# New tables for a hand-ordered attention and SwiGLU kernel: order, banks, buffers and block kinds

## The chip, the cores and the metric

The kernel runs on one core of a Trainium2 chip. The core has five engines that run side by side, each through its own instructions in their own order: TensorE (PE in the profile; its weight loads are a row of their own, PEld), VectorE (DVE), ScalarE (ACT), GpSimd (POOL) and SyncE (SP), which here only issues transfers. They wait for each other through semaphores. Matmuls write PSUM, 8 banks of 128 x 512 fp32 words; POOL doesn't touch PSUM here. The metric is the device time of one execution in microseconds; a kernel's time is the median of its runs.

## The reference

An attention block with 32 inducing points over x (4 batches of 12,416 rows of 128 channels), then a SwiGLU feed-forward block with RMS norm over all 49,664 rows, d_ff = 1536, everything in fp32:

```python
def mab(q, kv):
    s = scale * (q @ kv.transpose(0, 2, 1))
    s = s - s.max(-1, keepdims=True)
    a = np.exp(s)
    a /= a.sum(-1, keepdims=True) + 1e-09
    return a @ kv
h = mab(I, x)                      # I: 32 inducing rows
x = mab(x, h).reshape(B * S, D)
...
rms = np.sqrt(np.mean(x * x, axis=-1, keepdims=True) + 1e-06)
xn = x / rms * rms_g
g = xn @ w_gate
silu = g * (1.0 / (1.0 + np.exp(-g)))
val = xn @ w_val
return (silu * val @ w_out).astype(np.float32)
```

## The kernel before

**Tiling.** A batch is cut into 7 sets of rows, six of up to 2,048 rows and a rest of 256. A set makes four units (the last set one), so there are 25 units to a batch and 100 in all: 80 of 512 columns, 16 of 480 and 4 of 256. The feed-forward part takes each unit through 12 blocks of 128 of the 1,536 hidden columns, 1,200 blocks. Since the second attention's output is a combination of 32 rows, the gate and value weights are first multiplied with those rows; a gate is then one matmul of the stack `sg` with the unit's attention weights `a` (L720), a value one with `sv` (L748).

**A block.** After gate and value, ACT takes the silu (L730) and DVE the product u (L762). Then u is projected by `w_out`, and the letter of the block in the table `sorts` says how:

- P: the product is written to a buffer in SBUF and one fp32 matmul takes it with `wo` (L818; the profile has two records for it).
- S: the product stays in its PSUM bank. ACT makes a high half (L775), DVE a low half (L781), PE multiplies both (L806, L807) in fp32r, POOL adds the two halves in place (L826), and a third fp32r matmul takes the sum (L818).
- D: the product goes to SBUF, ACT makes the high half (L772), POOL the low half (L788), ACT scales the high half down (L794); from there on it is as S.

So P costs one fp32 matmul and nothing on ACT and POOL. The first two projections of a unit collect in one bank, the rest in another; at the unit's end ACT scales the one up (E, L850), DVE adds both (F, L859) and turns the result (T, L865), and SP stores it (O, L880).

**Work between.** The attention of the next batch (scores, exponentials, sums, norms: small matmuls L327, L380, L574 and pieces on all engines) and the splitting of `wo` run among the blocks: 879 such pieces. For each unit SP gathers `a` from the halves `hi` and `lo` by four transfers (L658) into one of two buffers.

**What sets the order.** No scheduler: the kernel runs under a manual schedule, and after a hand-written opening (`first()`, its own string ORDER) one string, `program`, is walked letter by letter. A letter issues one step: g gate, v value, s silu, m product, h high, l low, n and e the two steps of D, q the first two projections, d the add, r the third, p the plain projection, a the gather, E F T O the end of a unit, and a dot the next piece by its number in `taken`. The order of the letters is the order of the instructions on each engine's queue; semaphore waits are put in where data or buffers ask for them. Other tables give what a step uses:

- `banks`: the PSUM bank of each matmul group that opens one (2,707 digits);
- `holders`: which of 19 SBUF buffers a product or half is written to;
- `workers`, `outputs`: scratch and output buffers of the attention pieces and units;
- `picks`: where several blocks are ready for a step, which of them is taken (A the oldest);
- `sorts`: the kind of each block.

```python
for name in "".join(program.split()):
    step, args = micros[int(next(taken))] if name == "." else (do[name], ())
    in_turn(step, args, id(step) in alone)
```

Of the kernel before, what the change touches and what calls it, by code (L numbers as in the profile page):

```python
# [23 lines left out]
def kernel(  # L24
# [12 lines left out]
    m = inducing.shape[0]  # L37
# [1220 lines left out]
    def seams():  # L1258
# [13 lines left out]
        5674130256174302653024631602314062310426304162403164026143614302614076214076241036421635260135215603251032512034  # L1272
        5704571042751407523071207310273610276037231627361237013125317247315472150732457125321627536751671236153076513750
        7453451401743052173021735203105705635761760345701547341725702754751047624752370250240542764207560274602174603241
        0217413720546130173051354731703105340571245743673741534367317451267345173461540635613465036154025360432473604727
        0326473261032451605315432463165345276135276135261302601521045165412605264712615246512346521365134526261742601761
        6476201760314270152670524215460245601462135426172436524356124361256134513041035431743517053147037215702170251075
        2674152061274016274016741360713460735140753470254027430723405237020325103203651306521036501620137632431471673123
        6714261670416071504650147514061705642076442034270634207342106321642654235415246532013426031476320763476327064730
        2407230724571437542375142361725375603265103512635026514356031540514675064716501457261724721347261762347162341726  # L1280
        4315643764175610456740132657425764073475345605743650465635031036213251023561703214703475423541305423410654312657
        1643726254632675043742761320614272076471240762406275025472412754173514732512417236124126013264106413624013260170
        6512052761072615072156047214076041743046301367204163216305164654163405163456034576453676534726732574621736275327
        5632563275630216735216302563042150425341052731402531503561026135601236521053245415375241372157431502347570526730
        7536257230652643720413713024037210732471360417630756034540547360543765473267326516571352631075620753245236752437
        6254726342532617301750215621562701250172472401724740371231745027153025673165713051706314507614521404706427014267
        0132704152734527305427304637401256430242341021642361203467341263567517273276531762157036173510365436453140346521
        0341063426712637471426314753164370467136017314036437014703763470243724530734025403257124031234026304632614201423
        6501236047123640723403216234063451673513571567415376413257463521365032162136520165027301706412461741607261072640
        2310742123417341724357124504235142513425164256312574627356024370653047607640375630417045123014521342053126543054  # L1290
        1025745120571412046517604650645076037435043674265720751025615760127510651624756427432576437246537605234653062501
        2306105630246130561735120352063615326143045367436174571345143653712451721724512172014051732410241076103740137163
        4760516470617506270624754704326750365102571370215317207530724302630726037240673245620235062352031026305601253702
        5603672324037463276103412073157412574027120542571602670526375236502765326503715623457617267412542675102745217341
        0314024723107614027164516710612571721067521350263060564234520426730567305273571607516730167350143602156401630320
        3241063247012640162
    """
    workers = """
        20120102102102010120120201201201201201212120120102011021010210210
# [5 lines left out]
        abcdefghiacbedfghiacjklmbdnoegpqfirshacjklmbdgeifacnohpqbilmrsdgjknpefalqomcrjhbiskdgnlapqefoscbnkhriamjdplqogrs  # L1305
        pnfebchaqlkmijpdnogfersqkljmhbpanqiokdrselmjpnqoklfgjcbnphodralqismjknpeorgblqjksmfcnpdolqrijkshnaepolqgmjrkfsnc
        lbiqpomjrdelghaqpcfiksnjrbdhlomnrjaksfqplomncrjgkislbqpmoenkrjdqslpnhmfkacoqsrjmgnklpibsrjemoqndksrljpmoqfhnksrj
        lmapogqsrmcnjpbolkqsnreijomlkpqdhsanrjfcgbiqmeklhpocsdngbrajsiqhmklrepocfnjdbasigecnjqmdklbrposfqamhnkgjlrpcqoes
        njklmqdifbarogpsnlmqjkhrposenlidmqcrpfbosnmglqharjepkfinmcodbpkgsrahefjlqopinbcgsmajrhfqkdolcnjrpasoehbqmgiflkcd
        njrseoqahpmbilkncgdjoqrfsphmnabilkjeoqrspmnlkjogcrdhspfbqmnkaijslorpecqmhfgnrdkpqjabmslonireqckjlpdmofsnhqkgjrbl  # L1310
        apmioqcsknjlrpmdfoqshnjkeglpbsrminaocdfkjhlqspbrmoegdkjnsplrqimhkopjlfcmrnqaskobdlpnjqsmogknrljqepmosikrlhnpcmoa
        jsfqkrnplbmodgejichrsfqnakmbpegolcjqnkrsmpholijrqsnamdepgkobjlfnrcmpjlkhiqsemoanjrkpqlsmognldbsrfckjpqmonlshirka
        jepqmogfsnrcldpkqjmbsrnloqpijskmrnlpaohegqjcdrkonfmsbilpoaehgqjnrfbkmcsoilqjpkmdgsolqnejkpmhrnsoalpqjcmkigrnfesl
        dbhopmqjkarcslgniopfjkedslmqhrnopagjkmbqrcinsfdlojpagqrhkmenscijploqrbfnsdakghicmloebjnfpsadqkrmhljionpgfcqsekrd
        amlhjoibnpfqscekrmldgjonpqsahmlkribfjoqcnsepmlkrdgjoahqnfsrbljokpmqinsecorlkdjpamnqhlfjsgbkoemrpqcinljadskhfgeom
        bcirpqndlskjogqmnrecpkalojsbnrqhpfkmidlognprjcseqakmnplobqsirfdjghalekobmncpjdqsrkoilmgnpjqbrsokfnhpacledimrnsjq
        pokmrlnskmpojqgrnlksmbjpqrfonhlkcadesjpmqrloikngsjbplmqfhroknpmaqsjlrkonpmqsjlodrecinpqmjsklgrjfbosaqhcnmpklrjie
        nqmogdfpskjlcmbonqrkaphlmqerjiosgnkpqldfbcrmojpihlnsqgekrmojpacdfblnsqmokjrphlnsigkqjmloernpsdabjcfhlogiemkdhqrf
        jnpsclogaqremkbjlnodpihfsjqlrpcamkensbojirqfhlpojmkrnqsgoldjpcermankbfijrpmhgqsdoaenlckjbrpmqinsfdlogkjhrpnscmqa
        lobefkjrpinsdmrqpkjlohmrgnsqlpkojnabecmsrojpikqdnlmsrfkhojpnqmrslojkgpnbqrlsomjkcpanlsqeorimjfkpndshoqmlbrkjngps  # L1320
        cameoqplsjifrndhoqkpbmlrsgncjmolkpaeqroslndjmkphqbroislkfnjpmgqroslknacjpmldkqeroisnjbphfgmlkraqsonpjkdrqsmlonpk
        jcrqinfeblposkmrjqnlhgadopskcrjblmqeofnispghkrljqmnaospdlcbjnkrqmoseilpjnqghfamkrojsbnlprmokqcdjiesparfnlmokqbsr
        jpmhognclkeafisqrjnpolbkmsdqcgriojslenapqrkmfhojbsndglpqrckmiojelahspnqrkmojblfsdgnpqmorckjshlinaepobrqmsndlfrqk
        jgcpmhoslnaeriqkbjoslfnrpdmqgksljhaopcmnrkqlesjiopbmnrkfqsgljmdcophnrlajkeqsiopmlbnrjgfhkqsopmcdalnieb
    """
    sorts = """
        PPPPPPPPPPPPPPPPPPPSPSDPDPDPPPSDPPPPPPDDPDPSSPDSPSSDDPDPPDPDSDPDPSPSSPSPSPSSSDSPPDPSSSPSSSPDSPSSSSDDPSSSDSSPSSSS
        SPSDPSSPSSDSSPSDSPPSSSDPDPPDPSSPSPSSSDPSSPSSPSSDSPSSDSSSSPSSDSPPSSSSPSSSSSDSSSSSPSSDSSSSDSSSSDSDDSDPSPSSPSSPSSDD
        PPPPSPDPSSPPSSSPSSSDSPSPSSSDSPPSSSSSDSDPPSPPDSDDPSPPSPPSPSPSPPPPSSSSDPDDPSPSDDPDPPDPDDSPDPPDSPPSSSDPPPSPSSSSSSSD
        SPPPSSDDSPSDPSDSPDSSSSSSDSPPSDSPSSPPSSSSDPSSSPSSDSSDPDSPSSPSDSSSPSSSDSSPSPSSSSSDSSPSPSSSSPSPDSSDPPDDPPSPSSPSDDSS  # L1330
        SSPDSSSPSSDPSPSSSPSPSDSSSPSSSDPSSSSSDPSSSSSSSSSSSSSSSSSDDPSSSPSPDSDPPSSSSPSDSPPSSSSSSPSSDSPPDDPPPSDSDSPSSSPPDSSP
        SSPDSDPPDSPSDPSPDPSSPSPPPSPPPSSSPDPSDSPSDDPDPDSPDPSPDPSPPSSSDPSPDPSSPSSSSPPSDPDSSSSDPSSPSDSSDDSPPSSPSDDPDPPSPSSS
        SSPDSPSSDSSPDSDSPSSSSDSSDPSSPSSPPSSSSSDSDPSSSPPSPSSSSSSSSSPSSSSPSDSPPPPPSSSSPSSDPSPSPSSSDSSSSSSSDDSSPSSSSSPPSSSD
        SSPSSSSSSSSSSSDDSSSDSSPSSDPSSSPPSPSSSSSDSPSSDSSDPDPPPSSPPSDSPPDSSPDSPPSDSDDPSSPPPSPSSSSSPSPSPPPSSPSSPSDPPSPSSDSP
        DPSPSDPSDPDPSPSSDSSPSSPSSSSPPSPSSSPSPSSSSSSSSSSPDSSSPSSSDSPPSSSSSDSSPDPSSSSSDPSSPSSPSSSPSPSSDSSPSSPSSSDSSSPSSSDP
        SPSSDPSSPSSSSSSSSSPSPSDPSSSSSSDSPSPSSSSDPSSSSSSSPSSSDPSSPDPSSPSSSSDPPSSPSSSSDSSSSSPPSSSSDSSSPSSSPSSSSDPSDPSPPSSP
        SDSSSSSPSSSSDSSPSSPSSSSSDPSSPSSSSPSDSSPSSSSPSSSSDPSSPSPSDSPDSSSPSPSSSPPDSSDPPPPP
    """
    picks = """
        ABABAAAAAAAABABABAAAAAAAAAAAAAAAAAAAAAAAAAAAAAABAAAAAAAAAAADCABAAAAAAAAAAAAAAAAAAAAAAAAAAAAAAAABAAAAAAAAAAAAAAAA  # L1340
# [221 lines left out]
```

## Time and profile before

| | us |
|---|---|
| time, median of 3 runs | 1471.8 (1471.11 to 1471.89) |
| the profiled execution's own time | 1469.96 |
| its span, from the first instruction to the last | 1468.1 |
| mean granted TensorE clock | 0.999 |
| first gate of the blocks (L720) starts at | 41.5 |
| last matmul starts at | 1462.8 |

The profile is of one execution. The columns of the view of windows are the stretch, its length, and for each engine its busy time in it with its count of instructions, then the granted clock, the DMA engines' busy share and GB/s. A row of the view of groups gives line, engine, operation, what is written and read, and the count; behind the first bar the busy time in us and the mean ns of one, behind the second the idle time of the engine before it and what ended it. A row of the timeline gives start, duration, engine, line and operation; neighbours of one kind are merged, with their count. Matmul durations overlap, since matmuls are pipelined: the start of the next one shows what one costs.

### The profile page before, as it was taken

The numbers are of one execution on the slowest core, as the hardware profiler recorded it, in microseconds if no ns is written. First come the engines' busy times: TensorE is split into PE (matmuls) and PEld (weight loads), VectorE is DVE, ScalarE is ACT, GpSimd is POOL, SyncE is SP. The second block draws the span as 40 slices with busy tenths as digits, with TensorE's granted clock in tenths as the row PEclk, the third lists the DMA queues.
The fourth block names the chain that finished last, engine by engine and source line by source line (L and its number), as shares of the span: only waits on it lengthen the run. The fifth ranks groups of instructions, "written<-read, shape, count | busy, mean of one in ns | idle before, by whom it ended". The sixth has DMA issues, their size and how long they took to land.

```text
span 1468.1 us, 26087 instructions
## 1 busy us (share of the span) xinstructions
PE 1460.1 (99%) x7310; PEld 1106.3 (75%) x7310; DVE 1427.4 (97%) x2489; ACT 1304.2 (89%) x2607; POOL 1376.3 (94%) x1214
## 2 busy tenths in 40 slices
PE   9999999999999999999999999999999999999998
PEld 7557777877777777787777777787778777777787
DVE  7999999999999999999999999999999999999998
ACT  6798889889988988988999889898898899999987
POOL 2579998999999999899999999799999999999998
PEclk9999999999999999999999999999999999999999
DMA  7656224446444132726656221264322122212122
GB/s 283 137 95 126 55 55 87 113 104 119 90 87 84 25 67 47 150 48 139 112 106 118 39 42 37 49 130 98 62 57 54 33 37 44 39 38 40 37 43 34
DMA packets 391904, 116.02 MB, mean 79 GB/s; under 512 B 365648, under 2 KB 371280, under 8 KB 389200
## 3 DMA queue, kind: packets, MB, share of 16 engines
q1 hardware_dynamic: 391168, 114.28, 37.8%
q8 instruction: 58, 0.95, 0.3%
q14 instruction: 86, 0.70, 0.2%
q10 hardware_dynamic: 592, 0.08, 0.0%
HBM read 53.95 MB, written 27.00 MB: 55 GB/s over the span
## 4 chain that ended last, share of the span: by engine, by line
PE 98%; DVE 1%; ACT 0%; issue 0%; POOL 0%; POOLq 0%; DVEq 0%; ACTq 0%
PE gv L818 32%; PE gv L720 17%; PE gv L748 17%; PE gv L806 12%; PE gv L807 12%; PE gv L327 3%; PE gv L380 1%; PE gv L945 1%; PE gv L574 1%; PE gv L158 0%; PE gv L989 0%; PE gv L468 0%; DVE u L762 0%; ACT silu L730 0%; PE gv L1099 0%
## 5 line engine op out<-in xcount | busy, mean ns | idle before, releaser
L730 ACT ACTIVATE silu<-gv 128x512 f32<-128x512 f32 (+2 forms) x1200 | 675.2, 592 | 79.3 <-PE gv L720 62.7
L826 POOL TENSOR_TENSOR xn<-xn,xn 128x512 fp32r<-128x512 f32 (+2 forms) x468 | 580.7, 1257 | 23.0 <-PE gv L807 20.7
L720 PE MATMUL gv<-a,sg 128*128 128x512 f32 (+2 forms) x1188 | 478.4, 432 | 0.0
L748 PE MATMUL gv<-a,sv 128*128 128x512 f32 (+2 forms) x1188 | 449.4, 411 | 0.0
L762 DVE TENSOR_TENSOR gv<-silu,gv 128x512 f32<-128x512 f32 (+2 forms) x662 | 432.6, 673 | 6.1 <-PE gv L748 2.9
L775 ACT ACTIVATE xn<-gv 128x512 fp32r<-128x512 f32 (+2 forms) x643 | 376.2, 596 | 34.9 <-DVE gv L762 28.3
L762 DVE TENSOR_TENSOR u<-silu,gv 128x512 f32<-128x512 f32 (+2 forms) x538 | 343.1, 655 | 7.6 <-ACT silu L730 3.8
L818 PE MATMUL gv<-u,wo 128*128 128x512 f32 (+2 forms) x708 | 347.8, 577 | 1.2 <-DVE u L762 1.0
L781 DVE SCALAR_TENSOR_TENSOR xn<-xn,gv 128x512 fp32r<-128x512 f32 (+2 forms) x509 | 332.2, 662 | 5.1 <-ACT xn L775 3.0
L720 PEld LDWEIGHTS gv<-a,sg 128*128 128x128 f32 x1188 | 223.4, 189 | 102.2 <-issue 33.2
L748 PEld LDWEIGHTS gv<-a,sv 128*128 128x128 f32 x1188 | 223.0, 189 | 85.4 <-issue 23.1
L826 POOL TENSOR_TENSOR xn<-xn 128x512 fp32r<-128x512 f32 (+2 forms) x200 | 250.8, 1261 | 6.5 <-PE gv L807 6.2
L788 POOL TENSOR_TENSOR xn<-u,xn 128x512 fp32r<-128x512 f32 (+2 forms) x159 | 197.4, 1245 | 7.9 <-ACT xn L772 6.3
L826 POOL TENSOR_TENSOR u<-xn,u 128x512 fp32r<-128x512 f32 (+2 forms) x154 | 194.4, 1271 | 1.9 <-PE gv L807 1.7
L806 PE MATMUL gv<-xn,xn 128*128 128x512 f32 (+2 forms) x451 | 170.2, 378 | 0.0
L818 PEld LDWEIGHTS gv<-u,wo 128*128 128x128 f32 x708 | 132.0, 190 | 30.0 <-issue 12.0
L818 PE MATMUL gv<-xn,xn 128*128 128x512 f32 (+2 forms) x360 | 134.9, 385 | 0.0
L807 PE MATMUL gv<-xn,xn 128*128 128x512 f32 (+2 forms) x360 | 134.5, 374 | 0.0
L806 PE MATMUL gv<-xn,more 128*128 128x512 f32 (+2 forms) x347 | 131.3, 379 | 0.0
L772 ACT ACTIVATE xn<-u 128x512 fp32r<-128x512 f32 (+2 forms) x179 | 110.8, 620 | 9.2 <-DVE u L762 8.4
L794 ACT ACTIVATE xn<-xn 128x512 fp32r<-128x512 f32 (+2 forms) x179 | 112.1, 629 | 4.6 <-POOL xn L788 3.3
L818 PE MATMUL gv<-xn,more 128*128 128x512 f32 (+2 forms) x292 | 112.4, 393 | 0.0
(233 smaller groups left out, 1862.9 us busy)
## 6 DMA issues: line engine op xcount, KB each, us to landing
out_dram<-o SPq DMA_DIRECT2D x320, 64.0 KB, 2.0
xT<-in_x_dram SPq DMA_DIRECT2D x60, 256.0 KB, 4.5
xn<-in_x_dram SPq DMA_DIRECT2D x60, 256.0 KB, 5.2
a<-hi SPq DMA_DIRECT2D x152, 64.0 KB, 2.0
a<-lo SPq DMA_DIRECT2D x152, 64.0 KB, 2.0
xn<-in_x_dram SPq DMA_DIRECT2D x5, 1024.0 KB, 9.2
xn<-w SPq DMA_DIRECT2D x18, 256.0 KB, 4.4
out_dram<-o SPq DMA_DIRECT2D x64, 60.0 KB, 2.0
```

The lines of the kernel that those rows point to most:

```text
L720: nc.tensor.matmul(g[:, 0:T], stacks[b][0][:, ts(j, P)], halves_in_turn(one["a"][:, 0:T]), start=True, stop=True)
L730: nc.scalar.activation(sl[:, 0:T], gates.pop(n)[:, 0:T], AF.Silu)
L748: nc.tensor.matmul(v[:, 0:T], stacks[b][1][:, ts(j, P)], halves_in_turn(one["a"][:, 0:T]), start=True, stop=True)
L762: nc.vector.tensor_tensor(out=to, in0=sl[:, 0:T], in1=v[:, 0:T], op=ALU.mult)
L775: nc.scalar.activation(hi, t["u"], AF.Copy, scale=-(1.0 - 2.0 ** -13) * 2.0 ** -12)
L781: nc.vector.scalar_tensor_tensor(out=t["lo"], in0=t["hi"].bitcast(F32), scalar=4096.0, in1=t["u"], op0=ALU.mult, op1=ALU.add)
L788: nc.gpsimd.tensor_tensor(out=t["lo"], in0=t["u"], in1=t["hi"].bitcast(F32), op=ALU.subtract)
L794: nc.scalar.activation(t["hi"], t["hi"].bitcast(F32), AF.Copy, scale=-(2.0 ** -12))
L806: nc.tensor.matmul(to, weight_of(0, j), halves_in_turn(t["hi"]), start=not one["q"], stop=False)
L807: nc.tensor.matmul(to, weight_of(1, j), halves_in_turn(t["lo"]), start=False, stop=last)
L818: nc.tensor.matmul(to.rearrange("p (n h) -> p h n", h=2) if step2 else to, lhsT, rhs, start=one["left"] == NJ, stop=one["left"] == 1)
L826: nc.gpsimd.tensor_tensor(out=t["lo"], in0=t["hi"].bitcast(F32), in1=t["lo"].bitcast(F32), op=ALU.add)
```

## The change

Only tables change; no function does, nor the opening's ORDER. Compared place by place, these letters differ: `sorts` 32 of 1,200; `banks` 2,393 of 2,707; `holders` 2,082 of 2,207; `picks` 1,186 of 4,694; `workers` 41 of 65; `taken` 706 of 879; `program` 9,838 of 10,871; `outputs` none. The counts of the kinds go from 354 P, 662 S, 184 D to 371 P, 651 S, 178 D. `picks` other than A go from 482 to 865. The sequence of the attention's matmuls on PE and how many of them stand together stay as they were (90 matmul pieces in 53 runs), as does the number of changes between Exp and Silu on ACT (24).

```diff
     banks = """
-        5674130256174302653024631602314062310426304162403164026143614302614076214076241036421635260135215603251032512034
...
+        5674130257461207546740207562375627362703673026357032653260753265723652376513267312670361073631230476130417301472
...
     holders = """
-        abcdefghiacbedfghiacjklmbdnoegpqfirshacjklmbdgeifacnohpqbilmrsdgjknpefalqomcrjhbiskdgnlapqefoscbnkhriamjdplqogrs
...
+        abcdefghibacdefghibjkadelmcfghinoadbpqerscgihafbjkdlmcepqirsnoajlmghfpqdbckreisnahjogcmlpsebkqihrjdnofcgmlpsbenk
...
     sorts = """
-        PPPPPPPPPPPPPPPPPPPSPSDPDPDPPPSDPPPPPPDDPDPSSPDSPSSDDPDPPDPDSDPDPSPSSPSPSPSSSDSPPDPSSSPSSSPDSPSSSSDDPSSSDSSPSSSS
...
+        PPPPPPPPPPPPPPPPPPPSPPDPPPDPPPSDPPPPPPDDPDPSSPDSPPSPDPDPPDPDSDPDPSPSSPSPSPSSSDSPPDPSSSPSSSPDSPSSSSDDPSSSDSSPSSSS
...
     program = """
-        .gg.vs.vg.sgvs.gv.g......m.mspms...s....vv.mp.mpm.g...s..p..g.gsp.....g..gvp.ms.vvs....mp.msg.p....s.vv.vm.p....
-        g.mp..msv.p......gvvmsp.gmg.s...smp...vv....m..p.....ggsp....msvv...p.m.g..g.v..ps.s.av.g.mp.sm.gvm.h..s...l..m.
...
+        .gv.g..gv.s..smsv..gmvsggmvsp...p..v...m.gmsp...vgs.p...sv...pm....gp.s.g..m.mgsvp...s.p..mv.ggmvs..ms.p........
+        vp....mgv.sp.mvvgm..s..g.vv.sp...p...p.m.mg.gsp...mvsvg.g.sp....p..m..vm.v.gsg..pa.s.sgvm....h..ms..l..m..p...v.
...
     taken = """
-        114 4 116 1 0 62 24 88 115 5 87 25 2 3 8 50 26 9 28 6 27 51 113 29 118 53 12 63 52 54 55 10 64 16 30 119 89 11
...
+        115 1 62 116 24 88 0 2 117 8 25 5 120 4 50 26 6 27 3 9 29 28 51 12 30 53 52 113 54 63 114 40 55 64 10 59 65 89
...
```

More of the change, by code (lines that the diff above doesn't have):

```diff
@@ L1276 @@
[L1276 to L1285, printed above, removed]
@@ new lines @@
+        4162431502641506720162514571672142574162753126537253027506253053602540234621426312063120673167203716716425076425
+        0765204240645170263572031025712516270125746105201465314635124351265143256357362576053726072365706352403752305243
+        0514012450317234502375437652476325476352713406135061450614510346356243065264570467502467027467530542147107540270
+        5420174023047324607360472640730764103742025632764256746357421374267236073460324632710431204650435206352340623456
+        0263052537651326157261371453276527150261306315362503614216420160364701647316047603175303450347523502745302457320
@@ new lines @@
+        4701325737235712657342617035237540236037605320376350261370230243607264072653046730164201762012430610625306125046
+        2170215415710541243045370645710535436053401345601450260126316201321073210670326175213215724135723573251473215461
+        0263125360156310562137056235605163561641064350637540130673506306503762056257603524053725172353475132741254705347
+        0143701367014374160375461304257624352647325761437241354315230412341032543012546106170672604270146716230430720154
+        7021570452710746503425302463254302350462653407654071647376376417360137610326317657623761317645127463510375345714
@@ new lines @@
+        3701437105273140764204372137213470147213451341732163764325361475634132407263071603120175623170572034031401745043
+        1754601540751205761027561375310246371267206123061703627135726307450420607650476250746507215267243574365736272641
+        3256375217507653203276250347064750641736105304134365430514603645062456704602475240176450721725072350752701203521
+        7635170653476123076327641627312754607147104126014720642715604271407214037401372134720415201367326136023762037160
+        7162431242716726147625471271634576356137501370635721632067312043760432603204372306542751670562516725612051732670
@@ new lines @@
+        6254062507450620671427504765047652430647364270213074107450375104730435013750241043562134156431256125473257634503
+        7560346054075340760725017456142517256142376523642640726370537602751603750756037047657630734606510572167451674627
+        5421367546725367057640730536503475601532706271560251675602714607430147301763410764120437064375403450673047501674
+        0361073432640372405306357437216375234534751452437014731574561745317456345163407165031732176521720652147502415034
+        5730217015031230265734073502564053542356403160214517560750471576410364103541326503620315601365271023607243704064
@@ L1297 @@
+        0236740524357250673
     """
     workers = """
-        20120102102102010120120201201201201201212120120102011021010210210
+        20120201201201020120121021021020102012020201201201020120111201201
     """
@@ new lines @@
+        csmblkqnjopsfraligdkqmnehjrbfkopqclmagsjdbinrhfepqcksgjabdiolnmphekfcjgiebrpnqacskhmojedbrlifasphmocdfnqkjgrsilb
+        hadpmfoncrskqjleiphagdomrjnkfbqpslormceinjaqghkorsdfmlpqbinjekacromshnjglkpfmqrbsnopimcjldqaegrskmhfbopnjdilqrks
+        onegclbprqmhjsnoapdiflqkgcearjpdniemsokbcrljpnhqafmgrsonkleqmijprcdsbohjprsqkfmljnroasqpeigjkmnsbcpldrohqjksfpal
+        igecmdhbnrfokqcspjhefilomjqnspdkrlhaqgsnmobkpcfrleisjkmpnoqdrapbheslkjropncmqsfpgihklnrabjmosnepqdcifkhjralmpoqk
+        sjnbgdporfqlhkmnscieapqjogbdnhkrmpceqlaisjgnomfbpckehdarmgqslinbfhjoakpqrnmdsjolkngqhfsrecbmpjoiadgklnqsmfcrjopk
@@ new lines @@
+        lebinaghrqsmcodfihjpekliansbcormqhdjkflnpmgieoqlrasncbhdfipjgekolmarcdfpbigsqjnhlraskfipjecqnglhamsfroeipqbgkjln
+        cdmrapsqlfokjeibnghmpcdaqjrolksfbinmdhlrespqokcngidmjlkqbsrfholnaqkespmrcdiojnlhqksbfmgaedorchifnpsqilkjmodnchsg
+        aljqmbpofkrnisedlahqjbfmpkosrdcnlqgjkeohbmpisadcrqnefljibskmoprnqlgafhmjidosnkqprblcheaodmfrsjnqolkpimqhjbleonrk
+        mspqgcjlondmafhierkmsopqjglnbrkcqmosedpjlrfonqkpsmljrpisoqajhnkgbprmecfsqlojnkdispgbfmqjraklhcseifgpmonkjlsqprda
+        bolkmsqgnjioprfsqlkhcaonpregbslmiafqojpknhsdbemrjlqsknpmcogrjaklnqofhpesridbocaghnkfbjmgqlheposnakrbfqljmipkdogs
@@ L1383 @@
+        AAAAAAAAAAAAACCAAAAACAAAAAAAACAAAAAAABAABAAAAAABAAAAABAAAAAABABAAAAABAABAAAAABABAAAAAAAABABBAAACBBAAAA
     """
     program = """
[L1385 to L1387 removed]
@@ L1483 @@
+        shvmgrgsqmhdlphTsrdhgvlrOsqlgvgdqmqlsmvvEvdmrgvmsrhrmgsgpldhmslsqhvgqdhmqslgrhdrlsvqlvgdmqqmsvpFdrpmdTpvdpOmErrr
+        rpprFTO
     """
     taken = """
[31 rows of a table removed]
[31 rows of a table added]
     """
```

337 lines of the change are left out of this document (156 added, 181 removed), and 60 rows, old and new, of the table taken.

## The prediction

> **What bounds the kernel now.** I read the page's first lines, then one stretch of the windows view, from the first gate (41.5 us) to the last matmul (1462.8 us). What lies ahead is the opening, which the tables leave alone; behind it come the last unit's sum, transpose and store.
>
> ```profile
> span 1468.1 us, 26087 instructions
> PE 1460.1 (99%) x7310; PEld 1106.3 (75%) x7310; DVE 1427.4 (97%) x2489; ACT 1304.2 (89%) x2607; POOL 1376.3 (94%) x1214
> PE 98%; DVE 1%; ACT 0%; issue 0%; POOL 0%; POOLq 0%; DVEq 0%; ACTq 0%
> ...
> core 0: us, PE busy (x) PEld busy (x) DVE busy (x) ACT busy (x) POOL busy (x), PEclk, DMA share, GB/s
> 41.50:1462.80 1421.30, 1419.99 (x6840) 1074.76 (x6839) 1396.01 (x2393) 1277.55 (x2546) 1365.00 (x1187) 1.00 0.37 73
> ```
>
> PE is on 98% of the chain at a granted clock of 1.00, but DVE and POOL stand beside it at 97% and 94%. Busy time alone doesn't say whether PE streams or waits, since matmul ends are modelled. The starts do, so next comes the timeline of PE.
>
> ```profile
> 700.12 0.38 PE L720 MATMUL gv<-a,sg 128*128 128x512 f32 x1
> 700.34 0.38 PE L806 MATMUL gv<-xn 128*128 128x512 f32 x1
> 700.56 0.38 PE L807 MATMUL gv<-xn,xn 128*128 128x512 f32 x1
> 700.77 0.38 PE L818 MATMUL gv<-xn,more 128*128 128x512 f32 x1
> ...
> 702.28 1.02 PE L818 MATMUL gv<-u,wo 128*128 128x512 f32 x2
> 702.74 0.78 PE L818 MATMUL gv<-u,xn 128*128 128x512 f32 x1
> 703.36 0.38 PE L748 MATMUL gv<-a,sv 128*128 128x512 f32 x1
> ```
>
> A 512-column fp32r matmul starts (700.77 − 700.12) / 3 = 0.216 us after the one before. From 702.28 to 703.36 lie one plain block (the fp32 matmul with wo, two records) and one fp32r matmul: 1.08 − 0.216 = 0.86 us for the plain block. An S or D block sends three fp32r matmuls, 0.65 us. Narrower units I take by columns (480/512, 256/512).
>
> ```profile
> L720 PE MATMUL gv<-a,sg 128*128 128x512 f32 x948 | 386.0, 436 | 0.0
> L818 PE MATMUL gv<-u,wo 128*128 128x512 f32 x532 | 270.6, 594 | 1.2 <-DVE u L762 1.0
> L818 PE MATMUL gv<-u,wo 128*128 128x480 f32 x138 | 66.6, 566 | 0.0
> L818 PE MATMUL gv<-u,wo 128*128 128x256 f32 x38 | 10.7, 380 | 0.0
> ```
>
> With the widths (960, 192 and 48 blocks of 512, 480 and 256 columns; plain ones 266, 69 and 19, two records each) the block matmuls need 502.9 (gates and values) + 533.8 (S and D) + 292.6 (P) = 1329.3 of the 1421.3 us. The remaining 92 us hold the attention's matmuls and all of PE's waits. Going over all starts behind 41.5 us for those later than this spacing and the switches between tile shapes explain, I count 121 places with 11.2 us together, the first and the last of them here:
>
> ```profile
> 43.82 1.07 PE L327 MATMUL gv<-xT,hT 128*32 128x512 f32 x8
> 45.93 1.13 PE L818 MATMUL gv<-u,wo 128*128 128x512 f32 x2 [1.04 <-DVE u L762]
> ...
> 1462.77 0.19 PEld L818 LDWEIGHTS gv<-xn,more 128*128 128x128 f32 x1 [0.24 <-POOL xn L826]
> 1462.77 0.38 PE L818 MATMUL gv<-xn,more 128*128 128x256 f32 x1
> ```
>
> Sorted by what was late: 2.9 us in 26 places at the third matmul of a block (it waits for POOL's add), 2.2 in 20 at gates, 1.7 in 20 at values, 2.0 in 29 at the first two projections, 1.4 in 18 around plain blocks, and 1.1 in the row at 45.93. So PE streams for all but 0.8% of the span. **The change can gain 11.2 us at most, and pays from that whatever PE gets more to do.**
>
> **The change part by part.** *Block kinds.* Counting the letters: P 354 to 371, S 662 to 651, D 184 to 178; by width 13 more P at 512, 4 at 480, none at 256; by batch +8, +8, +2, −1. Each swap costs PE 0.86 − 0.65 = 0.21 us: 13 × 0.21 + 4 × 0.20 = **+3.5 us**, on the path, as nothing covers work on PE itself. The other engines are relieved, by these rows:
>
> ```profile
> L781 DVE SCALAR_TENSOR_TENSOR xn<-xn,gv 128x512 fp32r<-128x512 f32 (+2 forms) x509 | 332.2, 662 | 5.1 <-ACT xn L775 3.0 <-issue 0.2
> L775 ACT ACTIVATE xn<-gv 128x512 fp32r<-128x512 f32 (+2 forms) x643 | 376.2, 596 | 34.9 <-DVE gv L762 28.3
> L772 ACT ACTIVATE xn<-u 128x512 fp32r<-128x512 f32 (+2 forms) x179 | 110.8, 620 | 9.2 <-DVE u L762 8.4
> L794 ACT ACTIVATE xn<-xn 128x512 fp32r<-128x512 f32 (+2 forms) x179 | 112.1, 629 | 4.6 <-POOL xn L788 3.3
> L788 POOL TENSOR_TENSOR xn<-u,xn 128x512 fp32r<-128x512 f32 (+2 forms) x159 | 197.4, 1245 | 7.9 <-ACT xn L772 6.3
> L826 POOL TENSOR_TENSOR xn<-xn,xn 128x512 fp32r<-128x512 f32 (+2 forms) x468 | 580.7, 1257 | 23.0 <-PE gv L807 20.7
> ```
>
> DVE 11 × 0.66 = 7.3; ACT 11 × 0.60 + 6 × 1.25 = 14.1; POOL 11 × 1.26 + 6 × 2.50 = 28.8 us. None of it lies on the path by itself; it shortens the end only through PE's 11.2 us.
>
> *Weight.* The Trainium skill (TensorE: Matmul & The Clock Gate, section Back-to-back issue gap) gives about 131 ns per 512-column matmul in a sustained stream; a swap, one pass more, would cost 0.13 us by it and the 17 swaps 2.2. The rows above contradict it with 216 ns, so 3.5 stands.
>
> *Order, picks and buffers.* The list's order is the order on each engine. I measure a lead as the time that PE's entries between two places of the list take at the spacing above. The POOL add of a block (L826) stood closer to its third matmul than its own duration in 76 of 846 blocks; now in 25 of 829. The first plain block followed scores2 of set 1 directly; now seven gates and values stand between. A buffer of the 19 comes back to its next writer within 1 us of the matmul that last read it 293 times before, 181 now. Banks don't move: a silu, product, low half, scale_up or finish closer to the next matmul in its bank than its own duration 232 times before, 226 after (scale_up alone 2 and 8). High_down ahead of its projections gets worse, 9 short leads to 15.
>
> *What the waits become.* Row 45.93: its 1.1 us goes to 0 (DVE's product is covered by 7 × 0.216 = 1.5 us). Third matmuls: 2.9 × 25/76 = 1.0. For the other 7.2 us the bounds are 0 and 7.2 or more; I scale by the buffer leads, 181/293, to 4.5, since of their counts this one moves most; by the bank counts alone they would stay at 7.0. Sum 5.5, **a gain of 5.7 us**. What is late next is a gate or value behind its bank:
>
> ```profile
> PEld gv L720 <- ACT silu L730: 15.7, 62, 0.7
> PEld gv L748 <- ACT silu L730: 14.3, 60, 0.4
> PEld gv L818 <- POOL xn L826: 11.3, 36, 0.8
> ```
>
> These are idle times of the weight loads, most of it under a running matmul, so they order the causes and don't price them.
>
> *Table loads.* Going through ACT's entries for Exp and Silu, both lists change between them 24 times, in the same stages.
>
> ```profile
> L730 ACT ACT_TABLE_LOAD x12 | 15.4, 1283 | 1.3 <-PE gv L720 1.1
> L456 ACT ACT_TABLE_LOAD x8 | 10.3, 1283 | 0.1
> L358 ACT ACT_TABLE_LOAD x4 | 5.1, 1283 | 0.1
> ```
>
> 24 × 1.28 us before and after: nothing.
>
> *Transfers.* SP's queue is reordered too. Loads of x for the next batch keep at least 9 us ahead of their transposes. The gathers of a (L658, four transfers) are the exception:
>
> ```profile
> L658 SPq DMA_DIRECT2D a<-hi x192: 507/581/2702, 105.6 to 1439.9; - x192
> DMA to landing us min/median/max: 1.8/2.0/7.9
> ```
>
> Three issues of 0.58 and a landing of 2.0 make 3.7 us. Before, one gather of 98 had less than 6 us to its unit's first gate, now nine have 5.0 to 6.0. I take nothing for it, as 5.0 covers 3.7; the bound on the other side is the longest landing, 1.7 + 7.9 = 9.6, some 4 us late each.
>
> *Sum.* 1468.1 + 3.5 − 5.7 = 1465.9 us of span. This profiled execution took 1469.96 with its 1.9 us around the span, and the median of the runs, 1471.8, lies 3.7 above the span: **1469.6 us**, 0.15% below. A measurement of this kernel tells about 0.2% (2.9 us) from no change, so I forecast no change.
>
> **The rivals.** *Nearly all waits go.* If the relief on POOL and ACT frees the banks as well, some 2.5 of the 11.2 us stay: 1468.1 + 3.5 − 8.7 + 3.7 = 1466.6. For it: every lead count but two falls. Against: the bank counts hardly do. It decides from 6.5 us of waits gone; all gone gives 1464.1, the lowest possible.
>
> *PE isn't full.* PEld is busy 1074.76 of 1421.30 us; if the missing quarter were room, the extra passes of the 17 blocks would run in it and 3.5 would fall out: 1466.1. Against: a load takes 0.19 of the 0.216 us of a matmul, and the two loads of a plain block 0.38 of 0.86, so a full PE shows about this share with this mix. The Trainium skill (Perfetto Trace Analysis, section Identifying the Most-Contended Engine) states the rule behind it, that the busy share of weight loads measures PE's headroom and matmul busy time doesn't; by it the 76% here leave room, and the starts disagree.
>
> *The gathers arrive late: slower.* Place: the first gate of the nine units. If their four transfers take 6.2 us rather than 3.7, because an issue ahead of them on SP waits, PE stands 0.7 us at each: 9 × 0.7 = 6.3, and 1469.6 + 6.3 = 1475.9. It decides from 5.1 us of such waits (0.57 each). Everything on SP queues behind a gather that waits for its buffer, and the stores behind that. Speaks for it: the longest issue 2.70 and landing 7.9 us; against: the medians.
>
> **How the numbers follow.** Forecast 0.40 (its own range 1468.9 to 1474.7, where 7.0 of the other waits stay or a few gathers slip); waits gone 0.33; PE not full 0.05; gathers late 0.22. So faster 0.38, same 0.40, slower 0.22. The range goes from the floor, 1464.1, up to 1476.2, where all 11.2 us of waits stay (1475.3) or the gathers take 6.2 us; about 0.13 lies above it and little below.
>
> **What would show it.** PE should have 34 more wo records, at L818, and 17 fewer at L806; POOL's busy time should be 29 us smaller, ACT's 14. The wait of L818 on POOL L826 should shrink to a third and the one at the first plain block vanish. If gates of a fresh unit wait for DMA, the third rival holds; if PE's late starts stay near 11 us, the leads were not what mattered; if they sum to under 4, the first rival holds. A span that falls although PE's late starts stay would make the sum wrong from the ground up.

## The result, and the profile after

The changed kernel takes 1468.81 us (median of 18 runs, 1467.97 to 1470.39) against 1471.09 us for the kernel before in the same session (18 runs, 1470.27 to 1472.77): ratio 0.9983, 95% interval 0.9976 to 0.999. It is 2.3 us faster. The interval leaves out 1, so the gain is real; at less than 0.2% it lies inside what the prediction called no change. The forecast was 1469.6 us, reckoned from 1471.8 us for the kernel before.

The first lines of the page of the changed kernel and its chain of waits by engine, and behind them the stretch from the first gate to the last matmul in the windows view:

```profile
span 1467.2 us, 25908 instructions
...
PE 1460.5 (100%) x7293; PEld 1109.9 (76%) x7293; DVE 1424.0 (97%) x2478; ACT 1297.0 (88%) x2584; POOL 1351.5 (92%) x1191
...
PE 99%; DMA 0%; DVE 0%; issue 0%; ACT 0%; DVEq 0%
```

```profile
42.79:1461.82 1419.03, 1419.01 (x6823) 1077.21 (x6822) 1392.63 (x2382) 1270.36 (x2523) 1340.29 (x1164) 1.00 0.37 73
```

The span fell by 0.9 us, the stretch by 1421.25 − 1419.03 = 2.2 us: the first gate starts at 42.79 instead of 41.52. I don't count that 1.3 us to the change: the profiled runs of the experiments below, whose tables leave the hand-written opening alone too, have their first gate anywhere from 41.6 to 42.75 us, those that begin with the list of before (kinds_only at 42.75) as well as those that begin with the changed one (more_plain at 41.7). So the stretch is what is compared from here on.

How much of the stretch PE loses is read with one sum. Going down the list, I add up PE's work at the spacings of the prediction (0.216 us for a pass of 512 columns, 0.86 for a plain block, the attention's matmuls at their usual time) and subtract it from the time at which each matmul starts, with the first gate at zero. What grows is **PE's time beyond its stream**: waits, what a wait costs behind it, and odd switches between tile shapes.

| time, us | before | changed |
|---|---|---|
| 60 | 2.7 | 1.4 |
| 100 | 5.2 | 2.6 |
| 160 | 6.5 | 3.7 |
| 500 | 12.1 | 8.0 |
| 1000 | 18.6 | 13.5 |
| end | 23.9 | 18.2 |

At the end it falls by 5.7 us. The change in the stretch is that, with the plain blocks against it: −5.7 + 3.5 = −2.2. Half of it, some 2.8 us, is won before 160 us. The late starts, counted as in the prediction, went from 11.2 us in 121 places to 5.2 in 59: third matmuls 0.7, gates 1.4, values 1.2, first two projections 1.5, plain blocks 0.5.

The place of the first plain block, in the timeline of the changed kernel:

```profile
44.01 1.07 PE L327 MATMUL gv<-xT,hT 128*32 128x512 f32 x8
45.01 0.48 PE L748 MATMUL gv<-a,sv 128*128 128x512 f32 x1
...
46.19 0.38 PE L748 MATMUL gv<-a,sv 128*128 128x512 f32 x1
46.43 1.98 PE L818 MATMUL gv<-u,wo 128*128 128x512 f32 x4
```

The plain block starts 0.24 us behind the value ahead of it, where a pass takes 0.216: the 1.04 us of before are gone. The groups of instructions and the waits of the weight loads answer to those shown before:

```profile
L818 PE MATMUL gv<-u,wo 128*128 128x512 f32 (+2 forms) x742 | 364.6, 577 | 0.0
```

```profile
PEld gv L748 <- ACT silu L730: 11.8, 44, 0.8
PEld gv L720 <- ACT silu L730: 9.7, 40, 0.6
PEld gv L818 <- POOL xn L826: 5.4, 22, 0.4
```

The wo records are 742, 34 more than the 532 + 138 + 38 of before. The weight loads' wait on POOL's add is halved (11.3 to 5.4 us, where a third was forecast), and no gate of the changed kernel waits for a gather. The longest late start of a block's matmul is 0.33 us.

### The profile page after: what moved, and what is told of

It reads as the page before. It is cut to its first block, busy times and chain, and to the rows that moved or that the text cites. A ratio compares the mean times of both kernels' runs of the same rounds, so it can differ in the third digit from the quotient of the medians.

```text
span 1467.2 us, 25908 instructions
## 1 busy us (share of the span) xinstructions
PE 1460.5 (100%) x7293; PEld 1109.9 (76%) x7293; DVE 1424.0 (97%) x2478; ACT 1297.0 (88%) x2584; POOL 1351.5 (92%) x1191
## 4 chain that ended last, share of the span: by engine, by line
PE 99%; DMA 0%; DVE 0%; issue 0%; ACT 0%; DVEq 0%
PE gv L818 33%; PE gv L720 17%; PE gv L748 17%; PE gv L806 12%; PE gv L807 12%; PE gv L327 3%; PE gv L380 1%; PE gv L945 1%; PE gv L574 1%; PE gv L989 0%; PE gv L468 0%; PE gv L158 0%; PE gv L490 0%; DMA ind<-in_inducing_dram 0%; PE gv L567 0%; PE gv L1099 0%
## 5 line engine op out<-in xcount | busy, mean ns | idle before, releaser
L826 POOL TENSOR_TENSOR xn<-xn,xn 128x512 fp32r<-128x512 f32 (+2 forms) x379 | 469.8, 1251 | 19.2 <-PE gv L807 15.6
L720 PE MATMUL gv<-a,sg 128*128 128x512 f32 (+2 forms) x1188 | 462.3, 414 | 0.0
L775 ACT ACTIVATE xn<-gv 128x512 fp32r<-128x512 f32 (+2 forms) x608 | 354.6, 593 | 30.6 <-DVE gv L762 24.8
L818 PE MATMUL gv<-u,wo 128*128 128x512 f32 (+2 forms) x742 | 364.6, 577 | 0.0
L781 DVE SCALAR_TENSOR_TENSOR xn<-xn,gv 128x512 fp32r<-128x512 f32 (+2 forms) x445 | 291.6, 662 | 6.7 <-ACT xn L775 5.1
L826 POOL TENSOR_TENSOR u<-xn,u 128x512 fp32r<-128x512 f32 (+2 forms) x204 | 254.5, 1255 | 7.0 <-PE gv L807 3.7
L806 PE MATMUL gv<-xn,xn 128*128 128x512 f32 (+2 forms) x431 | 172.5, 400 | 0.0
L788 POOL TENSOR_TENSOR xn<-u,xn 128x512 fp32r<-128x512 f32 (+2 forms) x125 | 156.9, 1259 | 10.8 <-ACT xn L772 7.6
L818 PEld LDWEIGHTS gv<-u,wo 128*128 128x128 f32 x742 | 138.2, 190 | 29.5 <-issue 11.8
L806 PE MATMUL gv<-xn,more 128*128 128x512 f32 (+2 forms) x330 | 127.8, 387 | 0.0
L818 PE MATMUL gv<-xn,xn 128*128 128x512 f32 (+2 forms) x304 | 120.5, 404 | 0.0
L807 PE MATMUL gv<-xn,xn 128*128 128x512 f32 (+2 forms) x304 | 113.7, 374 | 0.0
L781 DVE SCALAR_TENSOR_TENSOR u<-xn,gv 128x512 fp32r<-128x512 f32 (+2 forms) x163 | 107.8, 666 | 1.6 <-ACT xn L775 1.0
L772 ACT ACTIVATE xn<-u 128x512 fp32r<-128x512 f32 (+2 forms) x166 | 103.0, 622 | 5.9 <-DVE u L762 4.3
L794 ACT ACTIVATE xn<-xn 128x512 fp32r<-128x512 f32 (+2 forms) x166 | 102.9, 623 | 4.9 <-POOL xn L788 2.9
```

Source lines behind the costliest of these rows:

```text
L720: nc.tensor.matmul(g[:, 0:T], stacks[b][0][:, ts(j, P)], halves_in_turn(one["a"][:, 0:T]), start=True, stop=True)
L772: nc.scalar.activation(hi, t["u"], AF.Copy, scale=1.0 - 2.0 ** -13)
L775: nc.scalar.activation(hi, t["u"], AF.Copy, scale=-(1.0 - 2.0 ** -13) * 2.0 ** -12)
L781: nc.vector.scalar_tensor_tensor(out=t["lo"], in0=t["hi"].bitcast(F32), scalar=4096.0, in1=t["u"], op0=ALU.mult, op1=ALU.add)
L788: nc.gpsimd.tensor_tensor(out=t["lo"], in0=t["u"], in1=t["hi"].bitcast(F32), op=ALU.subtract)
L806: nc.tensor.matmul(to, weight_of(0, j), halves_in_turn(t["hi"]), start=not one["q"], stop=False)
```

## The experiments

All are edits of the tables. In the short diffs below an entry of the list is its letter with the number of the block: q342 is "first two projections of block 342". Ratios are to the kernel before, measured beside each on the same chip. "Beyond" is the sum defined above at the end of the stretch, and the plain blocks' share is their number at 0.21 us (0.20 and 0.10 for narrower ones). The stretches are those of one profiled execution each. Differences of the median times to the same bases come out within 0.6 us of them (0.9 for late_gathers), so a few tenths of a us tell nothing.

| kernel | based on | plain blocks | beyond, us | stretch against its base, us | ratio, 95% interval |
|---|---|---|---|---|---|
| kinds_only | before | 354 → 372 | 23.9 → 23.7 | +3.4 | 1.0025 (1.0015 to 1.0034) |
| fewer_17 | changed | 371 → 354 | 18.2 → 44.5 | +23.0 | 1.0143 (1.0129 to 1.0157) |
| more_plain | changed | 371 → 416 | 18.2 → 27.4 | +18.7 | 1.0114 (1.0099 to 1.013) |
| third_later | before | 354 | 23.9 → 27.7 | +3.8 | 1.0028 (1.0018 to 1.0037) |
| buffers_far_before | before | 354 | 23.9 → 25.5 | +1.6 | 1.0012 (1.0003 to 1.0021) |
| buffers_far_after | changed | 371 | 18.2 → 19.6 | +1.4 | 0.9997 (0.9988 to 1.0006) |
| first_early | before | 354 | 23.9 → 24.4 | +0.4 | 1.0001 (0.9992 to 1.001) |
| swap_a | changed | 371 | 18.2 → 21.3 | +3.1 | 1.0006 (0.9997 to 1.0014) |
| opening_only | both | 358 | 22.2 | −0.9 to before | 0.9993 (0.9984 to 1.0002) |
| opening_back | both | 367 | 21.9 | +0.6 to before | 1.0002 (0.9993 to 1.0011) |
| spliced | both | 358 | 22.9 | −0.2 to before | 0.9999 (0.999 to 1.0008) |
| late_gathers | changed | 371 | 18.2 → 64.9 | +46.7 | 1.0294 (1.0276 to 1.0313) |

### The price of a plain block: kinds_only

```diff
  ... d340 g345
- h342
  q341 ... h344
- n342
  v346 ... n343
- e342
  v347 ... h346
- q342
  m348 ... h350
- d342
  g352 ... m351
- r342
+ p342
  g353 ...        (18 blocks in the same way; an S block loses its l in place of n and e)
```

> The kernel before with 18 of the 19 blocks that the change turns to plain (354 to 372 P) and nothing else moved. Theory (a swap costs PE 0.21 us, the relief of the other engines frees little): 18 x 0.21 = +3.7 us, 1474.8 us, ratio 1.0025; PE's late starts stay between 10 and 11.5 us. Rival (the relief of POOL and ACT is what takes the waits away): half of the 11.2 us goes, +3.7 - 5.6 = -1.9, 1469.2, ratio 0.9987. Rival (PE has room for the extra passes): no change or faster by the relief, 1469 to 1471.

Measured 1473.62 us beside 1469.86, ratio 1.0025, as the theory had it. Block 342 in the timeline of before, and then of this kernel:

```profile
471.56 0.38 PE L720 MATMUL gv<-a,sg 128*128 128x512 f32 x1
471.78 0.38 PE L806 MATMUL gv<-xn,more 128*128 128x512 f32 x1
472.00 0.38 PE L807 MATMUL gv<-xn,more 128*128 128x512 f32 x1
472.21 0.59 PE L818 MATMUL gv<-u,wo 128*128 128x512 f32 x1
...
477.71 0.38 PE L818 MATMUL gv<-xn,more 128*128 128x512 f32 x1
477.93 0.38 PE L720 MATMUL gv<-a,sg 128*128 128x512 f32 x1
478.14 0.38 PE L748 MATMUL gv<-a,sv 128*128 128x512 f32 x1
```

```profile
474.14 0.38 PE L720 MATMUL gv<-a,sg 128*128 128x512 f32 x1
474.36 1.02 PE L818 MATMUL gv<-u,wo 128*128 128x512 f32 x2
...
479.86 1.02 PE L818 MATMUL gv<-u,wo 128*128 128x512 f32 x2
480.32 0.78 PE L720 MATMUL gv<-a,sg 128*128 128x512 f32 x1
480.93 0.38 PE L748 MATMUL gv<-a,sv 128*128 128x512 f32 x1
```

Follow the distance between the two runs, with all else equal: 474.14 − 471.56 = 2.58 us, then 474.36 − 472.21 = 2.15, so the hole of the two projections closes by 0.43. At the value behind the plain block it is 480.93 − 478.14 = 2.79, 0.64 more. Net +0.21, the prediction's price. PE is full: neither a pass put in nor one taken out is absorbed. The 18 blocks' relief of POOL and ACT took away 0.3 us of waits by the profile, and nothing that the times show (3.76 us more for 18 swaps), not 5.6.

### The same from the other side: more_plain and fewer_17

```diff
(more_plain)   ... s537
- q532
  l534 ... d534
- r532
+ p532
  m540 ...        (h532, l532 and d532 go too; 45 blocks in the same way)
(fewer_17)     ... m743
+ h742
  s745 v744
+ l742
  v745 ... d737
+ q742
  g748 ... s747
+ d742
  p743 ... p739
+ r742
  T60 ... h747 .
- p742
  . l747 ...      (17 blocks in the same way)
```

> The changed kernel with 45 more S blocks of 512 columns turned to plain (371 to 416 P). Theory: 45 x 0.21 = 9.5 us on PE, less 0 to 1.5 us of waits that the relief takes away: 1476.8 to 1478.3, ratio 1.0039 to 1.0049. Rival (PE isn't full): the passes run in room that PE has, within 1 us of the changed kernel, 1468 to 1470, ratio 0.998 to 0.9993. By the Trainium skill (TensorE: Matmul & The Clock Gate, section Back-to-back issue gap), which gives about 131 ns for a matmul of 512 columns in a sustained stream, it would be an estimated 45 x 0.13 = 5.9 us, 1474.7.

> The changed kernel, its order kept, with 17 of its plain blocks turned to S (371 to 354 P, as many as before): 9 of 512, 6 of 480, 2 of 256 columns. Theory (order takes the waits away, the kinds only cost): 9 x 0.21 + 6 x 0.20 + 2 x 0.10 = 3.3 us less than the changed kernel, 1465.5, ratio 0.9962 to the kernel before; late starts of PE stay at 5 to 6 us. Rival (the plain blocks' relief of POOL and ACT is what the shorter waits live on): late starts go back to 8 to 11 us and the time to 1468.8 to 1471.5, ratio 0.9985 to 1.0003.

more_plain took 1486.72 us. Of its 18.7 us the plain blocks carry 45 × 0.21 = 9.5, as forecast; the other 9.2 are waits, where fewer were expected. Where two projections are taken from a place, PE runs 0.43 us early from there on. By the time the plain block came, 2 to 16 us later, the 0.43 was still whole to within 0.1 us at 16 of the 45; at the others PE had lost it in part or altogether to waits for what wasn't ready yet.

fewer_17 fell out wholly unlike the theory: its plain blocks give back 3.3 us, and 26.3 us of waits come. The rival was nearer and still too small. The largest are like this one, behind a low half that had been put in (block 748's):

```profile
966.00 0.82 PE L748 MATMUL gv<-a,sv 128*128 128x512 f32 x2
968.04 0.48 PE L748 MATMUL gv<-a,sv 128*128 128x512 f32 x1 [1.22 <-DVE u L781]
```

Six of the waits of over 0.3 us stand between 612 and 692 us. In a window of that stretch DVE of the changed kernel was already busy 39.12 us of 40:

```profile
620.00:660.00 40.00, 40.00 (x231) 32.26 (x230) 39.12 (x66) 35.48 (x72) 38.19 (x31) 1.00 0.43 100
```

An S block brings DVE 0.66 us and POOL 1.26 more, and neither has that much free for a long while, so all that stands behind comes late. My way of putting the steps in was rough. So this shows that the list as it stands has no room for 17 more S blocks, not that another list with 354 plain blocks couldn't have it; the kernel before is such a list, 5.7 us of waits above the changed one.

### The leads at the third matmul: third_later

```diff
  ... .exp1_of
- r136
  l146 g149 .sum_h
+ r136
  F11 s147 ...     (62 blocks in the same way)
```

> The kernel before with 62 third matmuls (L818, S and D blocks) moved later in the list, each at least 1.9 us of PE work behind its POOL add where it had less than the add's 1.25 us; the rest untouched. Theory: PE's late starts at third matmuls go from 2.9 us to 0.5 or less, those elsewhere stay: -2.4 us, 1468.7, ratio 0.9984. Rival (the wait only moves: buffers come back later, and gates and projections wait in its place): late starts stay at 10 to 11 us in all and the time at 1470.6 to 1471.5, ratio 0.9997 to 1.0003.

1474.01 us beside 1469.86: slower, against the theory and worse than the rival. Only 8 of the 64 blocks with a lead under 1.25 us for 512 columns (the prediction's 76 are those under 1.29) had waited at their third matmul before, by the late starts, so there was little to win: the moved ones went from 0.62 us to 0.31. And new waits came, above all here. PE and then DVE of this kernel, and DVE of before:

```profile
234.17 1.95 PE L380 MATMUL gv<-xn,e 128*32 128x128 f32 x64
236.06 0.48 PE L818 MATMUL gv<-xn,more 128*128 128x512 f32 x1
236.38 0.38 PE L748 MATMUL gv<-a,sv 128*128 128x512 f32 x1
237.42 0.45 PE L818 MATMUL gv<-xn,xn 128*128 128x512 f32 x1 [0.66 <-DVE o L859]
```

```profile
236.58 0.69 DVE L859 TENSOR_TENSOR o<-gv,o 128x512 f32<-128x512 f32 x1 [1.71 <-PE gv L818]
```

```profile
234.52 0.68 DVE L859 TENSOR_TENSOR o<-gv,o 128x512 f32<-128x512 f32 x1
```

Block 136's third matmul, the last of its unit, moved behind the 64 small matmuls of a sum. So DVE's finish waits 1.71 us for it with all of DVE's work behind, and the next unit's third matmul waits for the bank that this finish reads.

### The buffers: buffers_far_before and buffers_far_after

```diff
(holders, the first 60 letters, before)
- abcdefghiacbedfghiacjklmbdnoegpqfirshacjklmbdgeifacnohpqbilm
+ abcdefghiacbedfghiacjklmbdnoegpqfirshacjklbdegifachmndopfeql
```

> The kernel before, list and kinds and banks untouched, only the buffers of the 19 dealt out again: each writer takes the one that has been free longest. A buffer comes back within 1 us of its last matmul 36 times in place of 293 (181 in the changed kernel). Theory (the buffer leads carry the waits at gates, values and projections, as the prediction scaled them): 7.2 x 36/293 = 0.9 of the 7.2 us stay, -6.3 us, ratio 0.9957. Rival (the buffers don't decide; the order on the engines does): late starts of PE stay at 9.5 to 10.5 us and the time within 0.7 us of the kernel before, ratio 0.9995 to 1.0005.

> The changed kernel with its buffers dealt out in the same way (181 short returns become 112). Theory: the 4.5 us of waits scaled to buffers go to 4.5 x 112/181 = 2.8, -1.7 us against the changed kernel, ratio 0.9972 to the kernel before. Rival (buffers don't decide): no change against the changed kernel, ratio 0.998 to 0.9988.

1472.43 us beside 1470.86, and 1470.03 beside the same. With 36 short returns in place of 293, time beyond the stream rises by 1.6 us, where the theory had −6.3; in the changed kernel it rises by 1.4. Short returns of a buffer are not what PE waits for.

### The first plain block: first_early

```diff
  s1
+ m0
  g3 v2 s2 ... g5 (scores2 of set 1, four weight steps)
- m0
  . m1 s3 p0 ...
```

> The kernel before with the first block's product (L762) moved on DVE's list ahead of the opening's weight steps that stood before it, nothing else moved. Theory: the first plain block no longer waits, its 1.04 to 1.1 us at 45.93 goes and reaches the end whole: 1.0 us less, ratio 0.9993; what is late next is one of the weight steps behind it on DVE, 0.7 us later each. Rival (the time is only passed on, to the next gate or value that waits for a bank or to the opening's weights): PE's next late starts grow by as much and the end stays, ratio 1.0.

1470.88 us beside 1470.86, the rival's. The timeline of PE:

```profile
45.28 1.12 PE L818 MATMUL gv<-u,wo 128*128 128x512 f32 x2
47.85 1.12 PE L490 MATMUL gv<-xn,hg 128*128 128x512 f32 x2 [1.45 <-POOL xn L265]
```

The plain block follows scores2 at once, and the next small matmul waits 1.45 us for the opening's weights: DVE's steps for them had stood on the path. The wait at 45.93 was one of two, and DVE could serve only one of them first.

### Each late matmul by itself: swap_a

```diff
  h1060 v1064 v1065 s1065
- p1061
  l1062 d1059 h1063 m1064 g1067
+ p1061
  s1066 ...        (25 entries in the same way)
```

> The changed kernel with 25 matmuls that start late in its profile (0.05 to 0.33 us each, 2.9 us together) moved behind the next one or two entries of PE in the list. Theory (a wait is a matter of that place alone, and the next matmuls are ready): 2 to 2.9 us less than the changed kernel, ratio 0.996 to 0.997 to the kernel before. Rival (the matmul moved ahead waits as well, or what hangs on the delayed one comes late): within 0.7 us of the changed kernel or slower, ratio 0.9978 to 1.0.

1471.45 us beside 1470.86: 3.1 us more beyond the stream than the changed kernel, worse than the rival. The worst place, in the changed kernel and then in this one:

```profile
1315.63 1.02 PE L818 MATMUL gv<-u,wo 128*128 128x512 f32 x2
1316.42 0.48 PE L720 MATMUL gv<-a,sg 128*128 128x512 f32 x1
```

```profile
1317.30 0.64 PE L748 MATMUL gv<-a,sv 128*128 128x512 f32 x2
1318.58 0.48 PE L720 MATMUL gv<-a,sg 128*128 128x512 f32 x1 [0.63 <-ACT silu L730]
```

The plain block had started 0.06 us late, and it covered most of what the gate behind it waits for. Moved behind that gate it covers nothing, and the gate stands for the silu that frees its bank.

### Where in the list the gain sits: three splices

```diff
(opening_only)
- list = before
+ list = changed up to the gate of block 90, then what is left in the order of before
(opening_back)   the two exchanged
(spliced)        opening_only, and from the gate of block 816 on the changed kernel again
```

> A splice: the changed kernel's list, kinds, banks and buffers up to the gate of block 90 (160 us), from there the order and kinds of the kernel before (banks and buffers renamed at the seam). 358 P. Theory (half of the waits that go, 2.9 us by the time PE spends beyond its stream, lie ahead of 150 us, and they stay gone): -2.9 + 4 x 0.21 = -2.0 us, ratio 0.9986, about what the whole change gives. Rival (the list behind meets engines that are late, and takes the gain back): within 0.6 us of the kernel before, ratio 0.9996 to 1.0004.

> The splice the other way: the kernel before up to the gate of block 90, from there the changed kernel. 367 P. Theory: the 13 further plain blocks cost 2.7 us and the waits behind 150 us fall by 2.9: -0.2 us, ratio 0.9999; everything the change does behind the opening cancels out. Rival (the gain is spread over the list): 0.9983 to 0.999, as the whole change.

> The first splice with a second seam: behind the gate of block 816 (1030 us) the changed kernel again, whose waits fall there by 0.65 us at the same number of plain blocks. Theory: -2.0 - 0.6 = -2.6 us, ratio 0.9982, level with the changed kernel or 0.4 us below it. Rival (a seam costs more than it brings): slower than the first splice.

Time beyond the stream, along the kernel:

| time, us | before | changed | opening_only | opening_back |
|---|---|---|---|---|
| 160 | 6.5 | 3.7 | 3.7 | 6.5 |
| 300 | 7.9 | 4.6 | 5.0 | 7.7 |
| 500 | 12.1 | 8.0 | 9.7 | 11.8 |
| 1000 | 18.6 | 13.5 | 16.3 | 17.2 |
| end | 23.9 | 18.2 | 22.2 | 21.9 |

opening_only takes the opening's 2.8 us over whole and keeps 1.8 of them to the end; with four plain blocks more that is −0.9 us, between theory (−2.0) and rival, and 0.9993 can't be told from no change. opening_back wins 2.1 us behind the opening and pays 2.7 for 13 plain blocks; its 1.0002 agrees with "what the change does behind the opening cancels out". The two parts make 1.8 + 2.1 = 3.9 of the 5.7 us. Whether the rest is the price of the seams or belongs to the whole list isn't settled by these. A second seam (spliced) brought nothing. None of the versions beat the changed kernel.

### The gathers: late_gathers

```diff
  g767 l763 p756
- a63
  s767 d762 ... h775 r766 g777
+ a63
  h773 q768 ...    (21 gathers; this one from 14.7 to 3 us of lead)
```

> The changed kernel with 21 gathers of a (L658) moved later on SP's list, to leads of 5.5, 5, 4.5, 4, 3.5, 3, 2.5 and 2 us ahead of their unit's first gate, two or three of each; SP's stores and loads that they pass are issued ahead of them. Theory (a gather takes 3.7 us, as the prediction had it): no gate waits down to a lead of 4; 0.2 us each at 3.5, 0.7 at 3, 1.2 at 2.5, 1.7 at 2, in all 8.5 us against the changed kernel. Rival (the third of the prediction, 6.2 us to a gather): waits from 5.5 us on, 0.7 there and 4.2 at a lead of 2, some 50 us in all.

1514.06 us (2 runs): the time is the rival's, the place is not. Three first gates waited for their gather, 2.9, 1.8 and 0.7 us, at leads of 3.5, 5.5 and 5. The rest, and the most, came by another way. The wait of ACT's cast and the longest of PE, in the waits view, with the landings of the gather behind it, and then the timeline of SP, ACT and PE around the longest:

```profile
ACT hi L636 <- DMA a<-hi: 31.0, 5, 11.0
...
PE gv L806 <- ACT o L850: 10.3, 1, 10.3
...
DMA to landing us min/median/max: 5.8/7.0/8.0
```

```profile
986.97 1.97 SPq L880 DMA_DIRECT2D out_dram<-o  x4
989.03 3.69 SPq L100 DMA_DIRECT2D xn<-in_x_dram  x8
992.77 0.51 SPq L658 DMA_DIRECT2D a<-hi  x1
...
1001.25 0.62 ACT L636 CAST hi<-aT 128x512 fp32r<-128x512 f32 x1 [11.03 <-DMA a<-hi]
...
1002.42 0.79 PE L806 MATMUL gv<-xn,xn 128*128 128x512 f32 x1 [10.28 <-ACT o L850]
```

The gather stands behind four stores and eight loads on SP, 5.8 us of issuing, and its four transfers then take 5.8 to 8.0 us to land, where 2.0 is the median. It reads the halves `hi` of a set, and the cast that writes the next set's halves into the same buffer waits for it to land. That cast is on ACT, in order, with silus and the unit's scaling behind it, and these hold banks that PE needs.

The other moved gathers let their first gate start without a wait for a transfer, some with a list lead of 2 to 3 us. A lead counts PE's entries, but SP issues when its own queue and the buffer let it. For the gate at 644.51, with a list lead of 2, the first issue came at 639.47, 5.0 us ahead; for the one that waited 0.7 us, at 1251.01 with a list lead of 5, it came only at 1247.07, behind four stores.

## Why the prediction held, point by point

**The sum.** From the first gate to the last matmul it gives 1421.3 + 3.5 − 5.7 = 1419.1 us; the profile has 1419.03. The time came out 0.8 us under 1469.6, and 0.7 of that is the starting point: the kernel before took 1471.09 us in the later and longer measurement, not 1471.8. Against it the forecast was −2.2 us, and −2.3 came.

**Block kinds, +3.5.** Right in size and reason: −0.43 at the projections, +0.64 at the plain block, 0.21 a swap in kinds_only, so a pass costs its 0.216 us. The 131 ns that the Trainium skill (TensorE: Matmul & The Clock Gate, section Back-to-back issue gap) gives for it stand in no trace here. Relief was put at nothing for the path, and kinds_only shows 0.3 us at most. On the busy times it was half right: POOL fell by 24.8 us (29 forecast), but ACT by 7.2 (14). The durations of ACT's three lines (L775, L772, L794), added up over all their instructions in the two traces, do fall by 16.7; the page's busy time counts only once where neighbours overlap.

**The first plain block, 1.1 to 0.** Right in size at its place. The reason was incomplete: the wait goes only because the opening's weight steps are also placed anew, since in first_early the same 1 us comes up at the next small matmul. And the opening gave more than this row: 2.8 us by 160 us.

**Third matmuls, 2.9 to 1.0.** They fell to 0.7. The step that failed is the scaling "2.9 × 25/76": 8 of the 64 short leads wait, and curing 62 of them made the kernel slower. A number that fell for another reason came out near mine.

**The other 7.2, scaled by 181/293 to 4.5.** They are 1.38 + 1.17 + 1.46 + 0.49 = 4.5 us in the profile, and yet this is the weakest step: "since of their counts this one moves most" was a choice among counts, and with the count at 36 the waits didn't fall. The agreement is chance. What the runs put in its place: the waits go with the order on all engines at once. Of the nine kernels with one kind of edit, seven stand clearly higher beyond the stream than their base, by 1.4 to 47 us; first_early (0.4 higher) and kinds_only (0.3 lower) differ by no more than one profile can tell. That the change, which moves the whole list, lowers it by 5.7 fits this; which of its moves do it behind the opening stays open.

**The rivals.** "Nearly all waits go" wanted under 4 us of late starts, and 5.2 are left. "PE isn't full" fell with kinds_only and more_plain. "The gathers arrive late" didn't happen in the changed kernel, whose waits name no gather at a gate. But the argument against it, medians and "5.0 covers 3.7", was too thin: moved gates show waits at leads of 5 and 5.5, with 3.9 to 6.9 us from the first issue to the gate, while others with a lead of 2 don't wait. So the step that counted list leads for SP measured the wrong thing, and that nothing came of it in the changed kernel doesn't confirm it. Its price was too small as well, for it saw only the gate and not the cast that writes the halves.

## What to carry to other kernels

Where four engines stand at 88% of a span and more, the worth of a new order can be bounded from the late starts of the fullest engine, and each added pass costs its full length there; but a count of short leads doesn't say which of them wait, so test such a scaling by curing the count alone before trusting it. Before a wait is moved, look for what it covers: the entry behind it may wait for the same engine, or longer. For a transfer on an ordered queue count who overwrites what it reads, not only who reads what it brings.

## What the runs showed of the hardware

A wait can cost more than itself. Behind a matmul that starts late enough the next one is spaced wider, here in the kernel before (0.29 us late at 83.70):

```profile
83.19 0.40 PE L748 MATMUL gv<-xn,sv 128*128 128x512 f32 x1
83.70 0.48 PE L720 MATMUL gv<-xn,sg 128*128 128x512 f32 x1
84.02 0.38 PE L818 MATMUL gv<-xn,more 128*128 128x512 f32 x1
```

0.32 instead of 0.216 us, 0.10 more. Spacings of exactly 0.104 us too much stand 12 times among the late starts before, once after, 24 times in third_later and 33 in fewer_17. How late is late enough shows in fewer_17, among its fp32r block matmuls of 512 columns with others of their kind around them: all 14 that start 0.13 us late or more have it behind them, none of the 11 that start 0.03 to 0.125 us late (those late only by this 0.104 left out). In the kernel before 3 of 26 in that lower band have it.

In late_gathers the granted clock halves at long waits. Two waits of PE in its timeline, and then the granted clock (third last column) behind the first of them, behind the one at 1002.42 shown above, and behind the second:

```profile
243.31 0.45 PE L720 MATMUL gv<-a,sg 128*128 128x512 f32 x1 [1.62 <-DMA a<-lo]
...
1414.87 0.65 PE L720 MATMUL gv<-a,sg 128*128 128x512 f32 x1 [2.71 <-DMA a<-lo]
```

```profile
243.00:245.00 2.00, 1.69 (x7) 1.00 0.46 93
...
1006.00:1008.00 2.00, 2.00 (x5) 0.50 0.00 0
...
1416.00:1418.00 2.00, 2.00 (x4) 0.50 0.26 60
```

Behind 1.62 us of idle time the clock stays at 1.00. Behind 2.71 us it is 0.50 for some 3.5 us, and behind the 10.28 us at 1002.42 for some 6.4, with passes 0.43 us apart. PE's three other waits of over 2.7 us (3.95, 5.04 and 6.27 us) have half the clock behind them too. Half the clock for 3.5 to 6.4 us is 2 to 3 us lost. So in this trace a wait brings that much more with it from somewhere between 1.6 and 2.7 us on, and the third rival's "0.7 us at each" can't be carried on in proportion to longer waits. The Trainium skill (TensorE: Matmul & The Clock Gate, section Part 1: The HAM clock gate) has the clock halved after an idle window of about 3.4 us. The factor agrees with these rows; here 2.7 us of idle time were enough.
